# Turning two row groups by DMA transposes inside one shared SyncE queue

## Chip, cores and metric

One core of a Trainium2 chip. The metric is device time in microseconds (us) of one execution, the median of several. Engines: PE = TensorE, ACT = ScalarE, DVE = VectorE, POOL = GpSimd, SP = SyncE, which here only issues DMAs. A DMA issued by SP goes through SP's queue (q1 in the profile); one issued by POOL goes through a software queue (q0). The profile counts both against the same 16 DMA engines.

## The reference

```python
def _attn_ref(x, filt_r, filt_i):            # x: 8 x 3008 x 256, float32
    X = np.fft.rfft(x, axis=1)
    F = (filt_r + 1j * filt_i)[None, :, :]
    return np.fft.irfft(X * F, n=x.shape[1], axis=1)

def _moe_ref(x, w_in, w_out, beta):          # 24064 tokens, 256 -> 2048 -> 256
    h = x @ w_in
    g = h * (1.0 / (1.0 + np.exp(-beta * h)))
    return g @ w_out
```

A filter along the sequence, by Fourier transforms, and a two-layer network on its result.

## The kernel before

The transforms are products with small tables, in stages. The network runs in 47 blocks of 512 tokens, 16 steps each: a step is one block of 128 hidden features (`hps`, then ACT's swish `gT`, then `acc`). A first set-up brings batch 0 as far as step 0. The rest of batch 0 and the transforms of later batches are cut into units and put into the steps by `place(first, last, units)`. Each engine is given its instructions in this order, so a unit's place is also its place in every engine's queue.

Batch 0's result before the last stage is `z_t`; its rows have to be turned, in four groups of eight, before the last product (`last_z`). All were turned by PE:

```python
z_t = ypool.tile([P, NDC, J, KP], BF16, name="z_t", tag="y")
...
def turn_z(g, i, on_act=False):
    ...
    for e in range(4):
        for dc in range(NDC):
            nc.tensor.transpose(pz[:KP, e, dc*P:(dc+1)*P], z_t[:, dc, JG*g + 4*i + e, :], ident[:])
    evac(zz0[g][:, 4*i : 4*i+4, :], pz[:KP], on_act)
...
place(15, 29, uz(2, True))            # 2 turns, 4 products
units = uz(3, True)
place(20, 24, units[:2], per=2)       # group 3's turns
place(34, 58, units[2:])              # group 3's products
...
place(at + 1, at + 1, [lambda: a2_read(1)] + uf(JG, NK), per=9)  # 8 DMA transposes, 2 MB of filter
...
place(36, 36, ux(2), per=9)           # POOL: load x of batch 2 (16 KB rows)
at = place(52, 66, u1(2, True), per=3)  # its first use
```

Batch 1 goes another way: its first stage is turned by DMA transposes (`a2_read`), its later stage is written to DRAM (`d<-z` in the profile, from a `z` tile of which there are two) and read back turned (`zz_read`).

## Time and profile before

| | kernel before |
|---|---|
| median (and range) of 6 runs | 776.75 us (775.97 to 778.45) |
| PE busy, share of the span | 99% |
| PE transposes of `z_t` | 64, of which 32 for groups 2 and 3 |
| batch 2's x load issued | 81.73 us |
| first `d<-z` store issued | 79.58 us |
| step 48 starts on PE (first weight load) | 89.08 us |

The busy share is a first hint only.

### The profile page before, as it was taken

To read this page: it belongs to the slowest core of one execution; us is meant where nothing else is said; L and a number is where in the kernel's file an instruction comes from. 1 tells how busy PE (TensorE), PEld (TensorE's weight loads), DVE (VectorE), ACT (ScalarE), POOL (GpSimd) and SP (SyncE) were. 2 spreads that over 40 slices of the span, in tenths; PEclk is the share of its full clock that TensorE was granted. 3 is DMA by queue.
4 is the path that set the end of the run, shared out by engine and by line. 5 is a ranking of instruction groups with operands and counts; after the bars stand their busy time and mean duration, and the time that the engine had idled before them with its cause. 6 is when DMAs were issued, how large, how long until landed. Compare 5 with 4: busy or idle time off the path is not lost.

```text
span 775.3 us, 16219 instructions
## 1 busy us (share of the span) xinstructions
PE 767.5 (99%) x6444; PEld 554.2 (71%) x6444; DVE 379.3 (49%) x641; ACT 594.9 (77%) x926; POOL 142.8 (18%) x145
## 2 busy tenths in 40 slices
PE   8999999999999999999999999999999999999998
PEld 4877777777777777877768777787777776776665
DVE  7836846645446553474526735277353761401001
ACT  6888887886678867788677876778767787677776
POOL 7523401420013100231002410034000430000000
PEclk9999999999999999999999999999999999999999
DMA  7969755515911268022761237512451114100101
GB/s 170 240 164 191 169 164 106 136 55 155 177 43 68 89 145 161 30 85 85 160 134 47 78 116 146 106 64 80 130 110 55 49 69 129 56 28 28 55 28 55
DMA packets 103291, 80.48 MB, mean 104 GB/s; under 512 B 48466, under 2 KB 96996, under 8 KB 102258
## 3 DMA queue, kind: packets, MB, share of 16 engines
q1 hardware_dynamic: 100496, 63.73, 30.8%
q0 software_dynamic: 2720, 15.73, 10.5%
q8 instruction: 50, 0.82, 0.5%
q14 instruction: 25, 0.20, 0.1%
HBM read 46.15 MB, written 35.65 MB: 106 GB/s over the span
## 4 chain that ended last, share of the span: by engine, by line
PE 97%; ACT 1%; DMA 1%; POOL 0%; DVE 0%; issue 0%; POOLq 0%
PE acc L907 42%; PE hps L852 42%; PE ps L557 3%; PE ps L628 2%; PE ps L687 2%; PE ps L661 2%; DMA xg<-in_x_dram 1%; PE psz L477 1%; PE pz L549 0%; ACT a L109 0%; ACT a_t L109 0%; PE pb L403 0%; POOL xg L120 0%; PE ps L451 0%; PE ps2q L451 0%; PE pt L354 0%
## 5 line engine op out<-in xcount | busy, mean ns | idle before, releaser
L867 ACT ACTIVATE gT<-hps,beta_sb 128x512 bf16<-128x512 f32 x752 | 516.0, 688 | 166.8 <-PE hps L852 155.0
L907 PE MATMUL acc<-wout_sb,gT 128*128 128x256 bf16 x3008 | 451.6, 272 | 0.0
L852 PE MATMUL hps<-y,win_sb 128*128 128x512 bf16 (+8 forms) x1730 | 447.7, 351 | 0.0
L907 PEld LDWEIGHTS <-gT 128*128 128x128 bf16 x3008 | 279.6, 98 | 106.3 <-ACT gT L867 0.2
L852 PEld LDWEIGHTS <-win_sb 128*128 128x128 bf16 x1730 | 165.0, 98 | 24.4 <-issue 0.2
L677 POOL TENSOR_TENSOR v_t<-p_t,q_t 128x512 bf16<-128x512 f32 x84 | 106.7, 1270 | 383.9 <-DVE q_t L676 375.4
L111 DVE COPY ost<-acc 128x512 f32<-128x512 f32 (+2 forms) x89 | 56.6, 674 | 194.0 <-PE acc L907 188.4
L111 DVE CAST a<-ps 128x384 bf16<-128x384 f32 x96 | 53.5, 558 | 91.4 <-PE ps L628 91.2
L113 DVE TENSOR_SCALAR y<-ps 128x376 bf16<-128x376 f32 (+1 forms) x115 | 61.7, 544 | 59.5 <-PE ps L557 59.5
L672 DVE TENSOR_TENSOR p_t<-ps,frr 128x512 f32<-128x512 f32 x84 | 58.1, 692 | 33.5 <-PE ps L661 30.9
L676 DVE TENSOR_TENSOR q_t<-ps,fri 64x512 f32<-64x512 f32 x84 | 58.3, 694 | 1.2
L673 DVE SCALAR_TENSOR_TENSOR q_t<-ps,fri 64x512 f32<-64x512 f32 x84 | 57.4, 684 | 1.1
L557 PEld LDWEIGHTS <-zz 96*128 96x128 bf16 x512 | 35.3, 97 | 29.1 <-issue 0.3
L109 ACT ACTIVATE z<-ps 128x512 bf16<-128x512 f32 x84 | 49.6, 590 | 0.0
L628 PEld LDWEIGHTS <-xg 94*128 94x128 bf16 x448 | 30.7, 97 | 23.4 <-issue 0.4
L628 PE MATMUL ps<-t1b,xg 94*128 94x96 bf16 x448 | 36.7, 205 | 0.0
L557 PE MATMUL ps<-t,zz 96*128 96x94 bf16 x448 | 36.7, 204 | 0.0
L687 PE MATMUL ps<-v_t,t 128*128 128x256 bf16 x168 | 32.1, 273 | 0.0
L661 PE MATMUL ps<-a,t 128*128 128x256 bf16 x168 | 32.1, 273 | 0.0
L120 POOL DMA_DIRECT2D xg<-in_x_dram x22 | 12.1, 552 | 97.5 <-PE acc L907 93.9
L661 PEld LDWEIGHTS <-t 128*128 128x128 bf16 x168 | 15.7, 98 | 14.1
L687 PEld LDWEIGHTS <-t 128*128 128x128 bf16 x168 | 16.3, 98 | 6.4 <-DVE q_t L676 0.4
(118 smaller groups left out, 193.9 us busy)
## 6 DMA issues: line engine op xcount, KB each, us to landing
out_dram<-ost SPq DMA_DIRECT2D x80, 256.0 KB
d<-z SPq DMA_DIRECT2D x28, 384.0 KB
zz<-d SPq DMA_DIRECT2D x28, 384.0 KB
xg<-in_x_dram POOLq DMA_DIRECT2D x6, 1280.0 KB, 10.1
frr<-in_filt_r_dram SPq DMA_DIRECT2D x12, 256.0 KB
out_dram<-ost SPq DMA_DIRECT2D x20, 128.0 KB
frr<-in_moe_w_out_dram POOLq DMA_DIRECT2D x4, 512.0 KB, 12.8
xg<-in_x_dram POOLq DMA_DIRECT2D x6, 224.0 KB, 11.0
```

The lines of the kernel that those rows point to most:

```text
L111: nc.vector.tensor_copy(dst, src)
L113: nc.vector.tensor_scalar_mul(dst, src, scale)
L557: nc.tensor.matmul(ps[:, e, :NP], lhsT=zz[:, jj + e, dc * P : (dc + 1) * P], rhs=tab[:], start=True, stop=True,)
L628: nc.tensor.matmul(ps[:, e, :KP], lhsT=s["x"][:, 4 * jq + e, dc * P : (dc + 1) * P], rhs=t1b[:], start=True, stop=True,)
L661: nc.tensor.matmul(ps[:, e, :], lhsT=t2[:, k0 + e, 3:5, :].rearrange("p c k -> p (c k)"), rhs=s["a2"][g][:, :, kk + e, :], start=True, sto ...
L672: nc.vector.tensor_tensor(p_t[:], ps[:], frr[:, ks_, :], ALU.mult)
L676: nc.vector.tensor_tensor(q_t[:M], ps[M:P], fri[M:P, ks_, :], ALU.mult)
L677: nc.gpsimd.tensor_tensor(v_t[:], p_t[:], q_t[:], ALU.add)
L687: nc.tensor.matmul(ps[:, e, :], lhsT=t3[:, k0 + e, :], rhs=v_t[:, e, :], start=True, stop=True)
L852: nc.tensor.matmul(hps[:, pos - t0 : pos - t0 + ln], lhsT=win_sb[:, dc, fb * P : (fb + 1) * P], rhs=ys[b][:, dc, n0 : n0 + ln], start=(dc ...
L867: nc.scalar.activation(gT[:, :tn], hps[:, :tn], ACT.Silu, scale=beta_sb[:, fb : fb + 1])
L907: nc.tensor.matmul(acc[tb // per][:, tb % per, :], lhsT=g_[:, tb * P : (tb + 1) * P], rhs=wout_sb[:, f_, :], start=(f_ == 0 and tb % per = ...
```

## The change

The intent: 32 of PE's transposes move to the DMA engines, which have time to spare (q1 and q0 take 41% of it), and SP's queue is sorted so that everything arrives when it is needed. The core of the diff:

```diff
-    z_t = ypool.tile([P, NDC, J, KP], BF16, name="z_t", tag="y")
+    z_0 = a2pool.tile([P, NDC, JG, KP], BF16, name="z_0", tag="a2")
+    z_t = ypool.tile([P, NJG - 1, NDC, JG, P], BF16, name="z_t", tag="y")
+    gp.memset(z_t[:, :, :, :, KP:], 0.0)
 ... (each copy out of psz becomes two, one to z_0, one to z_t)
+    def read_z(g):
+        zz0[g] = zzpool.tile([P, NDC, JG, P], BF16, name="zz", tag="zz")
+        nc.sync.dma_start_transpose(
+            zz0[g].rearrange("p c j d -> p (c j) d"),
+            z_t[:, g - 1].rearrange("p c j r -> p (c j r)"),
+        )
 ...
-    place(15, 29, uz(2, True))
-    units = uz(3, True)
-    place(20, 24, units[:2], per=2)
-    place(34, 58, units[2:])
+    place(23, 30, uz(2, True))          # products only
+    place(48, 59, uz(3))
 ...
-        place(at + 1, at + 1, [lambda: a2_read(1)] + uf(JG, NK), per=9)
+        place(at + 1, at + 1, [lambda: a2_read(1, (0,)), lambda: read_z(2)], per=9)
+        place(at + 2, at + 2, [lambda: a2_read(1, (1,))], per=9)
+        place(19, 19, uf(JG, 2 * JG) + [lambda: a2_read(1, (2,))], per=9)
+        place(21, 21, uf(2 * JG, NK) + [lambda: a2_read(1, (3,))], per=9)
+        place(36, 36, [lambda: read_z(3)], per=9)
 ...
         place(36, 36, ux(2), per=9)     # unchanged
-        at = place(52, 66, u1(2, True), per=3)
+        at = place(56, 69, u1(2, True), per=3)
 ... (the last store goes out in two halves, from SP and ACT)
```

More of the change, by code (lines that the diff above doesn't have):

```diff
@@ L468, in inverse3 @@
         for j0, j1 in ((0, JG), (JG, J)) if last else ((0, J),):
-            nj = 4 * (j1 - j0)
+            ng = (j1 - j0) // JG
             if j0:
-                ps = fpsum.tile([P, 2, NDC, nj], F32, name="psz", tag="f")
+                ps = fpsum.tile([P, 2, ng, NDC, 4 * JG], F32, name="psz", tag="f")
             else:
-                ps = opsum.tile([P, 2, NDC, nj], F32, name="psz", tag="acc")
+                ps = opsum.tile([P, 2, ng, NDC, 4 * JG], F32, name="psz", tag="acc")
             for src, tab in ((p_t, t3), (q_t, t3b)):
@@ L477, in inverse3 @@
                         nc.tensor.matmul(
-                            ps[:, e, dc, :],
+                            ps[:, e, :, dc, :],
                             lhsT=src[:, e, dc * P : (dc + 1) * P],
-                            rhs=tab[:, k0 + e, 4 * j0 : 4 * j1],
+                            rhs=tab[:, k0 + e, 4 * j0 : 4 * j1].rearrange(
+                                "p (g r) -> p g r", g=ng
+                            ),
                             start=src is p_t and dc == 0 and e == 0,
@@ L484, in inverse3 @@
                         )
-            for e in range(2) if last else (None,):
-                if last:
-                    dst = z_t[:, :, j0:j1, 4 * (k0 + e) : 4 * (k0 + e) + 4]
-                    src = ps[:, e].rearrange("p c (j a) -> p c j a", a=4)
-                else:
-                    dst = z_t[:, :, :, 4 * k0 : 4 * k0 + 8].rearrange(
-                        "p c j (e a) -> p e (c j) a", e=2
-                    )
-                    src = ps.rearrange("p e c (j a) -> p e (c j) a", a=4)
-                evac(dst, src, not last or j0 > 0)
+            for e0, ne in ((0, 1), (1, 1)) if last else ((0, 2),):
+                cols = slice(4 * (k0 + e0), 4 * (k0 + e0 + ne))
+                if j0 == 0:
+                    evac(
+                        z_0[:, :, :, cols].rearrange("p c j (e a) -> p e (c j) a", a=4),
+                        ps[:, e0 : e0 + ne, 0].rearrange("p e c (j a) -> p e (c j) a", a=4),
+                        not last,
+                    )
+                if j1 == J:
+                    evac(
+                        z_t[:, :, :, :, cols].rearrange("p g c j (e a) -> p e (g c j) a", a=4),
+                        ps[:, e0 : e0 + ne, (JG - j0) // JG :].rearrange(
+                            "p e g c (j a) -> p e (g c j) a", a=4
+                        ),
+                        True,
+                    )
     def table4():
@@ L539 @@
     zz0[0] = apool.tile([P, NK * P], BF16, name="zz", tag="a1")
-    zz0[0] = zz0[0][:KP, : JG * D].rearrange("p (j d) -> p j d", j=JG)
+    zz0[0] = zz0[0][:, : JG * D].rearrange("p (c j d) -> p c j d", c=NDC, j=JG)
     def turn_z(g, i, on_act=False):
         if g not in zz0:
-            zz0[g] = zzpool.tile([KP, JG, D], BF16, name="zz", tag="zz")
-        pz = fpsum.tile([P, 4, D], BF16, name="pz", tag="f")
-        for e in range(4):
-            for dc in range(NDC):
-                nc.tensor.transpose(
-                    pz[:KP, e, dc * P : (dc + 1) * P], z_t[:, dc, JG * g + 4 * i + e, :], ident[:]
-                )
-        evac(zz0[g][:, 4 * i : 4 * i + 4, :], pz[:KP], on_act)
+            zz0[g] = zzpool.tile([P, NDC, JG, P], BF16, name="zz", tag="zz")
+        pz = fpsum.tile([P, NDC, 4, P], BF16, name="pz", tag="f")
+        for dc in range(NDC):
+            for e in range(4):
+                nc.tensor.transpose(pz[:KP, dc, e, :], z_t[:, g - 1, dc, 4 * i + e, :KP], ident[:])
+        evac(zz0[g][:KP, :, 4 * i : 4 * i + 4, :], pz[:KP], on_act)
+    def read_z(g):
+        zz0[g] = zzpool.tile([P, NDC, JG, P], BF16, name="zz", tag="zz")
+        nc.sync.dma_start_transpose(
+            zz0[g].rearrange("p c j d -> p (c j) d"),
+            z_t[:, g - 1].rearrange("p c j r -> p (c j r)"),
+        )
     def last4(zz, tab, jj, dc, dst, on_act, own=None, first=NP):
@@ L558, in last4 @@
                 ps[:, e, :NP],
-                lhsT=zz[:, jj + e, dc * P : (dc + 1) * P],
+                lhsT=zz[:KP, dc, jj + e, :],
                 rhs=tab[:],
@@ L586 @@
         if i % 2:
-            pz = opsum.tile([P, 2, D], BF16, name="pz", tag="acc")
+            pz = opsum.tile([P, NDC, 2, P], BF16, name="pz", tag="acc")
         else:
-            pz = fpsum.tile([P, 2, D], BF16, name="pz", tag="f")
+            pz = fpsum.tile([P, NDC, 2, P], BF16, name="pz", tag="f")
         for e in range(2):
             for dc in range(NDC):
-                nc.tensor.transpose(
-                    pz[:KP, e, dc * P : (dc + 1) * P], z_t[:, dc, 2 * i + e, :], ident[:]
-                )
-        evac(zz0[0][:, 2 * i : 2 * i + 2, :], pz[:KP], i % 2 == 1)
+                nc.tensor.transpose(pz[:KP, dc, e, :], z_0[:, dc, 2 * i + e, :], ident[:])
+        evac(zz0[0][:KP, :, 2 * i : 2 * i + 2, :], pz[:KP], i % 2 == 1)
     pw[0] = hpsum.tile([P, TB], F32, name="pw", tag="hps")
@@ L640, in s1, with a2_read @@
         )
-    def a2_read(b):
+    def a2_read(b, gs=range(NG)):
         s = st[b]
-        s["a2"] = []
-        for g in range(NG):
+        for g in gs:
             t = a2pool.tile([P, NDC, KG, P], BF16, name="a2", tag="a2")
@@ L651, in a2_read @@
                 )
-            s["a2"].append(t)
+            s.setdefault("a2", []).append(t)
     def s23(b, i):
@@ L697, in zz_read @@
         for h in range(NJG):
-            t = zzpool.tile([KP, JG, D], BF16, name="zz", tag="zz")
-            nc.sync.dma_start(t[:], s["d2r"][:, h * JG : (h + 1) * JG, :])
+            t = zzpool.tile([P, NDC, JG, P], BF16, name="zz", tag="zz")
+            t = t[:KP].rearrange("p c j d -> p (c j d)").rearrange("p (j c d) -> p c j d", c=NDC, j=JG)
+            nc.sync.dma_start(
+                t.rearrange("p c j d -> p j c d"),
+                s["d2r"][:, h * JG : (h + 1) * JG, :].rearrange("r j (c d) -> r j c d", c=NDC),
+            )
             s["zz"].append(t)
@@ L746, in uz @@
     def uz(g, act=False):
-        return [lambda i=i: turn_z(g, i) for i in range(2)] + [
-            lambda i=i: last_z(g, i, act) for i in range(2 * NDC)
-        ]
+        return [lambda i=i: last_z(g, i, act) for i in range(2 * NDC)]
     def uf(a, z):
@@ L774 @@
     place(0, 0, rest, per=9)
-    place(1, 14, uz(1, True))
-    place(15, 29, uz(2, True))
-    units = uz(3, True)
-    place(20, 24, units[:2], per=2)
-    place(34, 58, units[2:])
+    place(1, 14, [lambda i=i: turn_z(1, i, True) for i in range(2)] + uz(1, True))
+    place(23, 30, uz(2, True))
+    place(48, 59, uz(3))
     first_step = [(S * b // TB) * NFB for b in range(B + 1)]
@@ L921 @@
                     if last and h == nch - 1:
-                        for half in range(2):
+                        for half, eng in ((0, nc.sync), (1, nc.scalar)):
                             cols = slice(half * P, (half + 1) * P)
-                            evac(ost[:, c : c + per, cols], a[:, :, cols], half == 1)
-                    else:
-                        evac(ost[:, c : c + per, :], a[:], on_act)
+                            ost = pqpool.tile([P, 2, D], F32, name="ost", tag="pq"[half] + "_t")
+                            evac(ost[:, :1, :P], a[:, :, cols], half == 1)
+                            eng.dma_start(out[TOK - P :, cols], ost[:, 0, :P])
+                        continue
+                    evac(ost[:, c : c + per, :], a[:], on_act)
                     store(t0 + h * per * P, per * P, ost[:, c : c + per, :])
```

## The prediction

> **What bounds the kernel now.** I read the page first (busy shares, then the chain that ended last), then the chain in order of time, then the timelines of the TensorE (PE), ScalarE (ACT), VectorE (DVE), GpSimd (POOL) and SyncE (SP), and the DMA packets of single windows.
>
> ```profile
> PE 767.5 (99%) x6444; PEld 554.2 (71%) x6444; DVE 379.3 (49%) x641; ACT 594.9 (77%) x926; POOL 142.8 (18%) x145
> ...
> PE 97%; ACT 1%; DMA 1%; POOL 0%; DVE 0%; issue 0%; POOLq 0%
> ```
>
> PE is busy 99% and 97% of the chain that ended last is PE. Busy alone does not prove it, as matmuls overlap, so I took the distances between starts of successive matmuls in the timeline: 216 ns after one with 512 columns, 109 ns after 256, 55.5 ns after 128. Measured against these, PE loses 0.1 us or less in nearly every 20 us from 40 us to 766 us (0.4 us from 80 to 100). So after 40 us every PE instruction removed shortens the run by its distance, and every new wait of PE lengthens it. The set-up before (0 to 37 us) has gaps: DVE, ACT and PE take turns there.
>
> The transposes that go, in the chain in order of time (start us, us, what):
>
> ```profile
> 54.43 0.45 PE pz L549 x8
> ...
> 56.61 0.45 PE pz L549 x8
> ...
> 59.83 0.45 PE pz L549 x8
> ...
> 64.36 0.45 PE pz L549 x8
> ```
>
> Four packets of eight transposes, for row groups 2 and 3 of the first batch, each 0.45 us on the path. (Two more, at 37.9 and 39.7 us, belong to group 1 and stay.)
>
> SP's queue, and what stands around it, from the timelines (start us, us, engine, line, operation, tiles, count, idle before with releaser):
>
> ```profile
> 52.97 12.04 SPq L648 DMA_TRANSPOSE a<-a  x8
> ...
> 69.07 10.42 SPq L826 DMA_DIRECT2D out_dram<-ost  x10
> 79.58 7.49 SPq L692 DMA_DIRECT2D d<-z  x2
> ...
> 77.53 0.69 DVE L111 COPY ost<-acc 128x512 f32<-128x512 f32 x1 [2.37 <-ACT z L109]
> ...
> 80.52 1.27 POOL L677 TENSOR_TENSOR v_t<-p_t,q_t 128x512 bf16<-128x512 f32 x1 [3.93 <-DVE q_t L676]
> 81.73 1.10 POOL L120 DMA_DIRECT2D xg<-in_x_dram  x2
> ```
>
> Eight transposes of 128x768 hold SP 12.04 us (median 1.29 us each). Block 0's stores come only at 69.07, behind 2 MB of filter. DVE's copy at 77.53 is named as waiting for ACT; I read it as waiting for its buffer, because the 1 KB packets of block 0's stores leave the rings only at 76 to 78 us. That held up DVE, then POOL's v_t, then POOL's load of x for batch 2 at 81.73.
>
> The packets from 83 to 90 us:
>
> ```profile
> DMA packets 85, 1.34 MB, mean 192 GB/s; under 512 B 3, under 2 KB 3, under 8 KB 3
> ...
> q0 software_dynamic: 85, 1.34, 104.1%
> ```
>
> A d<-z store is issued at 86.73 in this window, yet no packet of SP's queue moves: the x load's 16 KB packets (1.23 us each) have all 16 engines until about 91 us.
>
> **What the Trainium skill says.** "DMA: Bandwidth & Descriptors", section "DMA Transpose (X-bar)": only SP and ACT can issue the transpose, the type must have two bytes, and two transposing streams must not be in flight together. The change keeps one stream, on SP; before has only SP transposes too, so the trace can't show the corruption. The same page, "Issuing engines are not separate DMA queues": all issuers share the same 16 engines. The trace agrees (85 packets of one queue, none of the other). "Queues, rings and completion order" there says an engine takes turns between rows packet by packet. The trace agrees in part: beside the x load at 192 to 199 us SP's queue gets single packets, beside the one at 83 to 90 us none. "TensorE: Matmul & The Clock Gate", "Part 4: PE-mode transpose", gives about 275 ns for one transpose in a kernel; here one lasts 219 ns but holds PE 55.5 ns, and the second number decides.
>
> **The change part by part.**
>
> 1. Removed: 2 groups x 8 rows x 2 halves = 32 PE transposes. 32 x 55.5 ns = 1.78 us (or 4 x 0.45), all on the path: **-1.8 us**. With them go four DVE copies of 0.69 us, off the path.
>
> 2. Added on SP: two transposes of 128x2048, 16 square blocks each. Six blocks take 1.28 us, so 16 take 3.4 us (estimate from that ratio). Nothing on PE.
>
> 3. z_t is split, z_0 on its own. Eleven ACT copies of 128x512 (594 ns) become 128x128 plus 128x384. The latter shape takes 491 ns; 128x136 takes 284 ns. So 594 becomes about 770 ns, +0.18 us x 11 = 1.9 us of ACT work between 21 and 35 us. ACT is nearly gapless from 22 to 30 us, but starts overlap their predecessor by 70 to 100 ns, so I count 0.1 us each, 1.1 us; ACT's own gaps between 27 and 34 us add up to more than that, and DVE sets the pace there, with results waiting for it some 0.3 to 0.6 us. I take **+0.2 us**. The memset of the padding (1536 elements a partition on POOL) falls in POOL's wait before 22.39 (1.57 us): 0.
>
> 4. Group 1's two transposed packets leave on ACT instead of DVE: two copies of 96x1024, about 1 us each (128x768 takes 0.82), at 39 and 41 us. ACT idles 1.38 us before 41.92 there, and PE has two hps banks: 0.
>
> 5. The end. Before, the last half copy on ACT waits for DVE's half (DVE 771.65, ACT 771.98) and one store follows at 772.28, SP being busy with the store before until 772.19. Now the halves go side by side and are stored from SP and ACT. Starts at about 772.0 and 772.2 instead of 772.28: **-0.1 us**. First use of ACT's queue is a small risk.
>
> 6. Order. Block 0's stores before the filter reload, the filter in two parts. All needs lie later than I place the landings: group 2 needed at step 23 (62.5 us before), issued 56.1 to 59.5; a2 of groups 1, 2, 3 at steps 29, 38, 47.
>
> Sum without new waits: 776.6 - 1.8 + 0.2 - 0.1 = **774.9 us**.
>
> **The rivals.**
>
> *A new wait for group 3.* This is the one I fear. Its transpose is placed at step 36, exactly where batch 2's x load is, and its reader at step 48, which starts at 89.18 before, so 87.4 after. SP now has to issue: transposes to 62.2, block 0's stores (3.6) to 65.9, filter and transposes twice (2 x 4.6) to 75.1, block 1's stores to 78.7, one d<-z, then the transpose from 79.3 to 82.7. If the x load keeps its place (81.7 - 1.8 = 79.9, packets 1.3 us later), most tiles go ahead of it and the wait is nil or short. But the stores' new place removes DVE's 2.4 us hold, so the load comes at about 77.5, with packets from 79 to 87, and the transpose is stuck. In before, where a transpose met such a load (issue 189.9 for the load, 191.86 for the transpose), twelve blocks were issued 12.8 us after the load's issue; for others about 11 to 11.5. Then sixteen land at 12 to 14 us after it, 89.7 to 91.5: PE waits 2 to 4 us, time 777 to 779. Against it: the reader's late place (48 to 59, was 34 to 58) looks chosen to avoid just this. I give a clear wait (over 1 us) one chance in three and charge its mean, about **+0.7 us**.
>
> *The set-up becomes ACT-bound.* All 1.9 us of point 3 on the path would cancel the gain: 776.6. For it: ACT without gaps from 22 to 30 us. Against: the gaps after. One in ten.
>
> *Transposes hidden anyway.* If PE had slack around 54 to 65 us, nothing would be won: 776.5. The distances between starts speak against it.
>
> **Range and chances.** 774.9 + 0.7 = 775.6; as the likelier case is the one without the wait, I predict **775.4 us**. Low end 773.8 (no loss in set-up, spread of 0.8 us between runs), high end 778.6 (the wait at 3.5 us). Two per cent is 15.5 us, several times anything here: faster 0.01, same 0.98, slower 0.01.
>
> **What would show it.** Right: transposes of z_t by PE fall from 64 to 32 and the chain is still PE without gaps from 40 us on; step 48 starts 1.8 us earlier than before; the set-up ends within 0.3 us of before. Wrong: PE idle before the first product of group 3 with the DMA of zz named, transposes of z_t on SP far over 3.4 us, the x load of batch 2 at 77 to 78 us; ACT named before PE between 24 and 34 us; the time from the last matmul to the end longer, not shorter.

## The result, and the profile after

The changed kernel takes 782.97 us (782.38 to 783.32, 6 runs) beside 776.75 us: 6.2 us longer. The ratio is 1.0076, 95% interval 1.0063 to 1.0089. (A ratio is the mean time of one kernel's fast runs over that of the other's fast runs of the same rounds, so not quite the ratio of the medians.) Both results are correct.

The page of the changed kernel, busy shares and the chain that ended last:

```profile
PE 762.3 (98%) x6310; PEld 553.7 (71%) x6412; DVE 376.9 (48%) x639; ACT 596.0 (76%) x935; POOL 144.5 (18%) x146
...
PE 94%; ACT 2%; DMA 2%; DVE 1%; issue 1%; SPq 0%; POOL 0%; DVEq 0%; POOLq 0%; ACTq 0%
```

PE weight loads fell from 6444 to 6412, the 32 transposes. (PE's own 6310 is lower still: some matmul records are missing from this trace, so I count steps by weight loads.) PE's share of the chain fell from 97% to 94%, and DMA's rose from 1% to 2%. The chain in order of time from 84 to 100 us shows which DMA came in (start us, us, what):

```profile
80.44 12.70 DMA zz<-z_t
93.13 0.05 issue
93.18 0.49 PE ps L573 x4
93.67 0.85 PE acc L925 x4
94.53 0.85 PE hps L870 x2
```

Group 3's transpose, issued at 80.44 us, lands at 93.13. PE had been ready since about 86.5. Two things are to be seen. PE waits, and then it is slow: four `acc` matmuls take 0.85 us where they took 0.44 before. The stretches around it, first of the changed kernel and then of the kernel before (span, then busy us and instruction count of each engine, granted PE clock, DMA share, GB/s):

```profile
86.00:93.00 7.00, 0.54 (x3) 0.04 (x1) 1.63 (x3) 1.19 (x3) 1.30 (x2) 0.90 1.05 240
93.00:98.00 5.00, 4.82 (x22) 2.91 (x23) 1.64 (x3) 1.89 (x4) 0.00 (x0) 0.50 0.09 35
```

```profile
86.00:93.00 7.00, 7.00 (x55) 4.95 (x54) 5.56 (x9) 6.20 (x12) 2.59 (x3) 1.00 0.93 198
93.00:98.00 5.00, 5.00 (x51) 3.58 (x50) 4.18 (x7) 4.54 (x9) 1.61 (x2) 1.00 0.40 130
```

From 93 to 98 us the granted clock is 0.50: 22 matmuls where 51 ran before. Who held the transpose up stands in the timelines of SP, POOL and ACT of the changed kernel:

```profile
75.05 4.01 SPq L844 DMA_DIRECT2D out_dram<-ost  x5
79.15 1.23 SPq L705 DMA_DIRECT2D d<-z  x1
80.44 10.66 SPq L565 DMA_TRANSPOSE zz<-z_t  x1
...
78.32 1.10 POOL L120 DMA_DIRECT2D xg<-in_x_dram  x2
...
91.46 0.60 ACT L109 ACTIVATE z<-ps 128x512 bf16<-128x512 f32 x1 [5.44 <-DMA d<-z]
```

Batch 2's x load was issued at 78.32, 3.4 us earlier than before, just ahead of `d<-z` and the transpose, which kept SP 10.66 us. In the packet records the load's 16 KB packets run from 79 to 88 us, `d<-z`'s from 87 to 91, most of the transpose's from 90 to 93. From 82 to 87 us the two queues pass packets one for one: 64 of the load beside 64 of 1 KB, the rest of block 1's stores, which stand ahead of `d<-z` and the transpose in SP's queue. And a second wait stands beside the first: ACT could not write its third `z` tile before the first had been stored, and stood still for 5.44 us.

The balance, by the first weight load of each step. The profiled changed kernel starts step 0 0.85 us ahead of the profiled one of before (the first x loads' arrival differs from run to run; in all traces step 0 starts between 35.8 and 36.8). At step 48 it is 3.24 us ahead: the 1.78 us of the transposes, and 0.6 us of work moved to later steps. From there to step 70 it falls to 6.36 us behind, a loss of 9.6 us. That is 6.7 us of waiting, 2.3 us of half clock, and the moved work.

### The profile page after: what moved, and what is told of

Its sections match the earlier page's. It is cut to its first block, busy times and chain, and to the rows that moved or that the text cites. A ratio compares the mean times of both kernels' runs of the same rounds, so it can differ in the third digit from the quotient of the medians.

```text
span 781.5 us, 16063 instructions
## 1 busy us (share of the span) xinstructions
PE 762.3 (98%) x6310; PEld 553.7 (71%) x6412; DVE 376.9 (48%) x639; ACT 596.0 (76%) x935; POOL 144.5 (18%) x146
## 4 chain that ended last, share of the span: by engine, by line
PE 94%; ACT 2%; DMA 2%; DVE 1%; issue 1%; SPq 0%; POOL 0%; DVEq 0%; POOLq 0%; ACTq 0%
PE acc L925 43%; PE hps L870 39%; PE ps L573 3%; PE ps L642 3%; PE ps L674 2%; PE ps L700 2%; DMA zz<-z_t 2%; PE psz L480 1%; ACT a L109 0%; PE pb L403 0%; ACT a_t L109 0%; ACT t L280 0%; ACT r L284 0%; PE ps L454 0%; ACT gT L885 0%
## 5 line engine op out<-in xcount | busy, mean ns | idle before, releaser
L870 PE MATMUL hps<-y,win_sb 128*128 128x512 bf16 (+8 forms) x1630 | 427.2, 350 | 0.0
L113 DVE TENSOR_SCALAR y<-ps 128x376 bf16<-128x376 f32 (+1 forms) x119 | 63.9, 545 | 66.9 <-PE ps L573 66.9
```

The lines of the kernel that those rows point to most:

```text
L113: nc.vector.tensor_scalar_mul(dst, src, scale)
L870: nc.tensor.matmul(hps[:, pos - t0 : pos - t0 + ln], lhsT=win_sb[:, dc, fb * P : (fb + 1) * P], rhs=ys[b][:, dc, n0 : n0 + ln], start=(dc ...
```

## The experiments

Ten runs, in three groups, each group on one chip with its own runs of the kernel before.

### Who makes PE wait: four runs (before: 776.16 us)

**e1_load44**: the x load alone is moved.

```diff
-        place(36, 36, ux(2), per=9)
+        place(44, 44, ux(2), per=9)
```

> Changed kernel, only batch 2's x load moved from step 36 to step 44. My theory (the load's 16 KB packets hold up SyncE's queue, first the d<-z store, then group 3's transpose): the transpose then issues in under 4 us at about 80 us and lands before step 48; neither TensorE's wait of 6.6 us nor ScalarE's wait of 5.4 us for d<-z is left, no stretch at half clock; 774.3 to 775.6 us, that is 1 to 2.4 us under the kernel before. Rival A (a transpose of 128x2048 is slow by itself, some 10 us): its issue stays near 10 us and the time near 783.

Measured: 779.34 us (777.13 to 780.77), ratio 1.0035 (1.0020 to 1.0051). The waits in question are gone and the time still is not what I expected. SP's and PE's timelines:

```profile
77.93 0.54 SPq L705 DMA_DIRECT2D d<-z  x1
78.52 3.22 SPq L565 DMA_TRANSPOSE zz<-z_t  x1
...
98.76 0.80 PE L642 MATMUL ps<-t1b,xg 94*128 94x96 bf16 x8 [2.99 <-DMA xg<-in_x_dram]
```

The transpose now takes SP 3.22 us and not 10.66, so rival A (slow by itself) falls. But POOL, in program order, issued the load only at 86.45, too late for its first use: a new wait of 2.99 us, again followed by a clock of 0.50 (from 99 to 103 us). The mechanism held; my estimate of when the load would be in did not. The six runs fall in two groups: three with a mean clock of 1.000 take 777.1 to 778.4 us, three with 0.995 to 0.998 take 780.3 to 780.8. The trace is of the second group, so whether the clock falls seems to decide some 2 to 3 us.

**e2_z3_early**: the transpose alone is moved, ahead of block 1's stores.

```diff
-        place(36, 36, [lambda: read_z(3)], per=9)
+        place(22, 22, [lambda: read_z(3)], per=9)
```

> Changed kernel, only group 3's transpose moved from step 36 to 22, ahead of block 1's stores; the load stays at 36. My theory holds two waits side by side: the transpose lands by about 78 us, but the first d<-z store is issued at about 80.7, behind the load, and lands near 90, so ScalarE's copy of z at step 47 still waits some 4 us and TensorE after it 2 to 4 us, perhaps with a cold clock: 778 to 781 us. Rival B (only the transpose's landing counts): 774.3 to 775.6. Rival A: about 783.

Measured: 783.93 us (783.51 to 784.34), ratio 1.0095. No wait for `zz` is left, but the kernel is no faster. ACT's timeline:

```profile
93.61 0.60 ACT L109 ACTIVATE z<-ps 128x512 bf16<-128x512 f32 x1 [6.81 <-DMA d<-z]
```

So rival B (only the transpose counts) falls. The number itself lies above my range and near rival A's 783, but the transpose kept SP 4.23 us and not 10, so it isn't A. A wait for `d<-z` suffices by itself: PE then waits 6.04 us for ACT's `gT`. It is not quite the wait of the changed kernel, and larger than I said, because the transpose and the stores it pushed back delayed `d<-z` to 83.5.

**e3_z3_pe**: group 3 is turned by PE again, at step 46.

```diff
-        place(36, 36, [lambda: read_z(3)], per=9)
-    place(48, 59, uz(3))
+    place(46, 46, [lambda i=i: turn_z(3, i, False) for i in range(2)], per=2)
+    place(48, 59, uz(3))
```

> Changed kernel, group 3 turned by TensorE again (at step 46), no second 128x2048 transpose. My theory: 16 transposes come back (+0.9 us), the wait for zz goes, but d<-z still sits behind the load (issued about 79.2, landed near 90), ScalarE waits about 4 us at step 47: 778 to 781 us. Rival B: 775.5 to 776.2.

Measured: 780.52 us (780.26 to 781.57), ratio 1.0057, as the theory says. ACT waits for `d<-z`, and PE for ACT's `gT`:

```profile
91.18 0.60 ACT L109 ACTIVATE z<-ps 128x512 bf16<-128x512 f32 x1 [4.04 <-DMA d<-z]
...
92.40 0.59 PE L870 MATMUL hps<-y,win_sb 128*128 128x512 bf16 x1 [3.27 <-ACT gT L885]
```

With no second long transpose at all, the new order of SP's queue beside an earlier load already costs more than the change can win.

**e4_warm**: useless work in the wait.

```diff
+    def keep_warm(n):
+        t = fpsum.tile([P, TB], F32, name="kw", tag="f")
+        for _ in range(n):
+            nc.tensor.matmul(t[:], lhsT=win_sb[:, 0, :P], rhs=win_sb[:, 0, :TB], start=True, stop=True)
+    place(48, 48, [lambda: keep_warm(28)], per=9)
-    place(48, 59, uz(3))
+    place(48, 59, uz(3), per=9)
```

> Changed kernel with 28 matmuls of 512 columns into an unused bank put into TensorE's wait at step 48 (28 x 0.216 = 6.0 us, the wait is 6.6). My theory: after the wait the changed kernel runs from 93 to 98 us at half clock, which costs 2.4 us (24 matmul distances of about 0.1 us more); with the array kept busy there is no such stretch: 780.2 to 781.0 us. Rival C (the half clock costs nothing that isn't made up): 782.5 to 783.3.

Measured: 780.71 us (780.34 to 781.22), ratio 1.0056. The transpose still holds SP for 10.75 us, but the clock after the wait stays at 1.00:

```profile
86.00:93.00 7.00, 6.88 (x35) 3.24 (x34) 2.07 (x3) 1.57 (x3) 1.81 (x2) 1.00 1.05 220
93.00:98.00 5.00, 4.36 (x37) 3.19 (x38) 3.11 (x5) 2.95 (x6) 0.00 (x0) 1.00 0.24 88
```

The profiled spans differ by 2.1 us (781.5 and 779.4). In both traces step 49 starts at 94.1 us; from there to step 52 the changed kernel takes 5.32 us and this one 3.21. So some 2 us of the loss is not waiting but the cold (halved) clock after it, and rival C falls. The changed kernel itself was not timed on this chip; the ratios to before (1.0076 and 1.0056) make it 1.6 us.

### Where the load should go: four runs (before: 775.98 us)

**f1_load39**: step 39, the first place at which the transpose should be through.

```diff
-        place(36, 36, ux(2), per=9)
+        place(39, 39, ux(2), per=9)
```

> Changed kernel, batch 2's x load at step 39 instead of 36. My theory: the d<-z store (issued about 78) and group 3's transpose (78.5 to 81.7) are through before the load's packets begin (load issued about 80.5 to 81, packets 1.3 us later), and the load is in by about 91, before its first use at step 56 (about 95). No wait of TensorE over 0.5 us between 40 and 100 us: 774.0 to 775.2 us, 0.9 to 2.2 under the kernel before. Rival D (SyncE's queue is too full whatever the load does): a wait of 1 us or more for zz, d<-z or a2 stays, 776 or more.

Measured: 794.32 us (793.24 to 794.64 in the fast runs, 812.42 in one slow run), ratio 1.0225. This is the worst of all. Rival D's words (a wait of 1 us or more, 776 or more) cover it, but not its size, and f2_load41 below removes the wait by moving the load alone. SP's timeline, PE's timeline, and the packets from 83 to 90 us:

```profile
79.55 8.83 SPq L565 DMA_TRANSPOSE zz<-z_t  x1
...
104.27 0.50 PE L573 MATMUL ps<-t4b,zz 96*128 96x94 bf16 x4 [17.52 <-DMA zz<-z_t]
```

```profile
DMA packets 376, 0.19 MB, mean 28 GB/s; under 512 B 370, under 2 KB 370, under 8 KB 370
...
q1 hardware_dynamic: 369, 0.09, 157.2%
q0 software_dynamic: 7, 0.10, 7.3%
```

The load was issued at 80.59, and its packets began at 83.4, when 1019 of the transpose's 2048 were through. From then on both nearly stop. In seven microseconds only 7 packets of the load run (85 in the kernel before), and 369 packets of SP's queue take 157% of all engines' time: in the records, 97 packets of 256 B, which last 0.018 us elsewhere, last 1.2 to 2.8 us, that is, as long as one or two of the load's 16 KB packets (1.23 us), or somewhat longer. And the load's packets start at 83.38, 84.61, 85.85, 87.08 and 88.32: one at a time, not one on each engine. It looks as if the transpose's packets go in step over the engines, so that one engine busy with the load holds the others. That became theory E, tested below.

**f2_load41**: the same diff with step 41.

> The same with the load at step 41. My theory: load issued about 83, in by about 93, just ahead of step 56: 774.0 to 775.6 us. If step 44's wait for x (3.0 us) is only a matter of the load's place, two to three steps earlier are enough; if the load itself has become slower beside SyncE's queue, TensorE waits for x again and the time is 776 or more.

Measured: 775.62 us (774.98 to 775.79, and one run of 781.22 with a mean clock of 0.995), ratio 0.9998 (0.9974 to 1.0022). The load is issued after the transpose:

```profile
80.10 3.11 SPq L565 DMA_TRANSPOSE zz<-z_t  x1
...
83.61 1.10 POOL L120 DMA_DIRECT2D xg<-in_x_dram  x2
```

What is left is about 1.3 us lost between the starts of steps 56 and 57, when x arrives.

**f3_z3pe_load39**: the edit of e3_z3_pe with the load at 39.

> Load at step 39 and group 3 turned by TensorE: group 2's DMA transpose alone. If a PE transpose is worth its 55.5 ns on the path, this lies 16 x 55.5 ns = 0.9 us over the run with the load at 39: 774.9 to 776.1 us.

Measured: 775.73 us (775.19 to 776.06), ratio 0.9988 (0.9973 to 1.0002). Within the expectation; but the run to which the 0.9 us was to be compared was the one that failed, so it says nothing exact of the worth of a transpose. It does show that the load at step 39 is harmless where no transpose is in flight.

**g_parts**: the rest of the change without its DMA transposes and without its order: `z_0` apart, new layouts, split last store; places, turns and queue order as before.

> Only the rest of the change on the kernel before: z_0 split from z_t, padding memset, new tile layouts, last store in two halves; all groups turned by TensorE and the old order and places. By my prediction's terms +0.2 - 0.1: 776.2 to 776.8 with the kernel before at 776.4. If ScalarE's added copies were on the path it would be 777.5 or more; if the split end were worth more than I think, 775.8 or less.

Measured: 776.54 us (776.04 to 776.91), ratio 0.9999 (0.9983 to 1.0015). These parts cost and win nothing that can be seen, to some 1.3 us either way.

### The step of the engines, and the version that wins: two runs (before: 776.48 us)

**h1_load41_u58**: load at 41, first use two steps later.

```diff
-        place(36, 36, ux(2), per=9)
-        at = place(56, 69, u1(2, True), per=3)
+        place(41, 41, ux(2), per=9)
+        at = place(58, 71, u1(2, True), per=3)
```

> Changed kernel, load of batch 2 at step 41 and its first use moved from step 56 to 58. In the run with the load at 41 alone TensorE still lost about 1.2 us between steps 56 and 58, the load being issued at 83.6 and in at about 94. Two steps later (96.9) it should be in: all 32 transposes' 1.8 us then count, 774.0 to 775.2 us, 0.9 to 2 under the kernel before. If it stays at 775.5 or more, something other than the load's arrival takes the rest.

Measured: 774.62 us (774.11 to 775.20, 6 runs), ratio 0.9968 (0.9949 to 0.9986). The gain of the medians is 1.86 us, near the 1.78 of the 32 transposes; that it is so near is partly luck, as the interval runs from 1.1 to 4.0 us and the profiled run is only 1.44 us ahead at step 80, counted from step 0. This version beats both kernels (the changed one by 8 us, on another chip).

**h2_plain_copy**: f1_load39 with a plain copy of as many 256 B pieces in place of the transpose (relative error 0.23). Its output is wrong, which doesn't matter for the time.

```diff
+    def copy_z(g):
+        zz0[g] = zzpool.tile([P, NDC, JG, P], BF16, name="zz", tag="zz")
+        nc.sync.dma_start(
+            zz0[g].rearrange("p c j d -> p (c j) d"),
+            z_t.rearrange("p g c j r -> p (g c j) r")[:, :: NJG - 1, :],
+        )
-        place(36, 36, [lambda: read_z(3)], per=9)
+        place(36, 36, [lambda: copy_z(3)], per=9)
-        place(36, 36, ux(2), per=9)
+        place(39, 39, ux(2), per=9)
```

> Wrong result on purpose. The run with the load at 39 (794 us), where group 3's transpose met the load in flight, but with a plain copy of as many 256 B pieces (16 a partition) in place of the transpose. Theory E (a transpose's packets go in step over all 16 engines, so that one engine serving a 16 KB packet holds the other 15; seen there as 256 B packets of 1.25 us and x packets one at a time): the plain copy lets the engines go their own way, x packets run 14 to 16 at a time, zz lands by about 92, TensorE waits at most 6 us: 776 to 785 us. Rival F (taking turns packet by packet with 16 KB packets explains the 17 us by itself): 791 to 796 us.

Measured: 784.74 us (782.58 to 786.40), ratio 1.0096. The packets from 83 to 90 us, and PE's timeline:

```profile
q0 software_dynamic: 106, 1.49, 109.8%
q1 hardware_dynamic: 356, 0.10, 6.1%
...
93.44 0.50 PE L580 MATMUL ps<-t4b,zz 96*128 96x94 bf16 x4 [6.61 <-DMA zz<-z_t]
```

About as many small packets in the same stretch now take 6.1% and not 157.2%, the load runs on (106 packets, not 7; thirteen start between 83.2 and 83.4 us), and PE waits 6.61 us, not 17.52, a little over what theory E said. Rival F, which wanted taking turns to explain all, falls. The split into 6.6 us for taking turns and 11 us for the transpose as such is only an estimate: the copy was issued faster (SP took 0.90 us), and half a microsecond after the load's first packet 255 of its 2048 packets were left, where the transpose had 1029. The difference in the load's own rate does not depend on that. That the engines wait for each other is the reading that fits; no record shows the hand-over between engines itself.

## Why the prediction was wrong, point by point

The time fell outside the range (773.8 to 778.6), 7.6 us above the point. The cause was on the list of rivals, and was given too little weight.

1. *Removed transposes, -1.8 us*: right. At step 31, when group 2's products are done in both kernels, PE is 1.87 us further ahead than at step 0, of which 0.09 is also in g_parts; with the waits cured the run is 1.86 us under before (h1_load41_u58, within its interval).
2. *SP's cost of 3.4 us for a transpose of 16 blocks*: 3.11, 3.15 and 3.22 us in three runs, but 1.60 us for group 2, 4.23 in e2_z3_early and 10.66 behind the load. The ratio from six blocks is only roughly usable.
3. *Set-up +0.2, end -0.1*: not distinguishable from nothing (g_parts). The reading of the end was wrong in part. ACT's half still starts only when DVE's has ended (778.40 and 778.08 in the changed kernel), so the old order did not come from the shared output tile. From the start of the last matmul to the store's last packet both kernels take 2.4 us.
4. *The new wait for group 3*: this is the step that failed, in three ways.
   - *Its chance.* My own sums said that the load would come at about 77.5 (measured 78.32), that the transpose would be issued from 79.3 (80.44) and land at 89.7 to 91.5 (93.13). I then set it at "one chance in three" because the reader's place at steps 48 to 59 "looks chosen to avoid just this". An argument from how a kernel looks outvoted the sums from the trace. It was wrong. A third of 2 to 4 us is also 0.7 to 1.3 us, so +0.7 was the least of it, and the high end of 778.6 lies below this rival's own 779.
   - *Its size.* "PE waits 2 to 4 us" was 6.6. I took the landing from transposes of before that had other stores ahead of them; here the rest of block 1's stores and a `d<-z` store stood between, whose packets took until 91 us. And step 48's first matmul came earlier (85.94) than the 87.4 I took it for.
   - *What follows it.* The half clock after the wait, some 2 us (e4_warm), was not in the sum at all, although "TensorE: Matmul & The Clock Gate" in the Trainium skill, Part 1, says that after an idle window of about 3.4 us the array goes down to half its clock and needs about as long to come back. This case agrees on the half clock (0.50 from 93 to 98 us). The times spread more: in the clock records of the six traces with a long wait, the clock falls 2.0 to 5.0 us after PE ran dry (2.0 in e1_load44, whose wait is 3.0) and is back 3.3 to 5.9 us after PE resumes. Each such stretch lasts a whole multiple of 3.41 us (3.41, 6.83, 10.24 or 20.48).
5. *Order of the queue*, "all needs lie later than I place the landings": wrong for `d<-z`. It is not a new transfer and I had looked only at new ones. Behind the earlier load it held up ACT 4 to 7 us and sufficed to lose the gain (e2_z3_early, e3_z3_pe). The filter's second part came late too: in the changed kernel DVE waits 2.75 us for it before 71.99, which PE did not feel. And where I read that none of SP's packets moved from 83 to 90 us before, none was waiting until the store of 86.73.
6. *DVE's hold at 77.53 is a wait for block 0's stores, and goes with the new order*: agrees. Before, the copy waits for the semaphores of the first two of block 0's stores among others, and these are done at 77.05 and 77.33. In the changed kernel the same copy starts at 74.12 without a wait, and the load moved up by 3.4 us. This rests on the two traces; no run changed that alone.

## What to carry to other kernels

When a queue is sorted anew, ask what each earlier finish will trigger: here block 0's stores left sooner, so DVE, then POOL and a 1.5 MB load moved up (as the two traces read), into the path of a store that nobody had touched and of the new transpose. In this kernel a bulk load did best behind the transfers that a reader waits for, and worst in the middle of a DMA transpose (775.6 us with the load after it, 783 ahead of it, 794 in its midst). Where PE sets the pace, count a wait of 3 us or more at its length plus the cold clock afterwards, here some 2 us after a wait of 6.6.

## What the Trainium skill lacked or had wrong

- "DMA: Bandwidth & Descriptors", "Rules for kernel authors": "A transpose next to ordinary DMAs needs nothing". True for the result, which was correct in f1_load39, but not for the time: 369 packets of SP's queue took 157% of the engines' time, and PE waited 17.5 us, beside 6.6 with a plain copy (which was further along when the load began).
- The same page, "Queues, rings and completion order", on turns packet by packet: it lacks that a queue's small packets can then move at the pace of the other queue's 16 KB packets of 1.23 us (64 beside 64 from 82 to 87 us in the changed kernel), and that a store that comes late waits longer still (before, issued at 86.73 us, its first packet at 90.52).
- The same page, on DMA transposes: SP's time for one of a given shape on this chip is not given; here 1.21 to 1.35 us for 39 of the 56 of 128x768 before, 1.6 to 4.2 us for 128x2048 with no load beside it, 8.8 to 10.8 us beside one.
- "TensorE: Matmul & The Clock Gate", "Part 4: PE-mode transpose": a duration of about 275 ns in a kernel. Here one lasts 219 ns, but in a full stream it holds PE only 55.5 ns.
